# Thirteen clock fillers in two groups instead of seventeen in four, and another order of the steps, in a kernel that fuses sketched attention with a rational feed-forward layer

## The chip, the cores and the metric

The kernel runs on one core of one Trainium2 chip. The metric is the device time of one execution in microseconds (us). Several runs of a kernel are summed up by their median. A profile of one execution shows, for each engine, when its instructions ran: TensorE (PE, with its weight loads as PEld), VectorE (DVE), ScalarE (ACT), GpSimdE (POOL) and SyncE (SP), which only starts DMAs here.

## The reference, cut to what matters

Each input row is turned by two small sketches (8 x 32) into the 64 products of its two sketch vectors. Attention with these features is linear, so keys and values are first summed into a 64 x 33 matrix for each head, and every query row is then one product with it and one division. The result, 4352 rows of 128, goes through a feed-forward layer whose nonlinearity is a quotient of polynomials.

```python
def _attn_ref(q, k, v, S1, S2):          # q, k, v: 4 x 4 x 1088 x 32
    def phi(x):
        a = np.einsum('rd,bhsd->bhsr', S1, x)
        b = np.einsum('rd,bhsd->bhsr', S2, x)
        return np.einsum('bhsi,bhsj->bhsij', a, b).reshape(*x.shape[:-1], r * r)
    q_p, k_p = phi(q), phi(k)
    kv = np.einsum('bhsf,bhsd->bhfd', k_p, v)
    z = np.sum(k_p, axis=2)
    num = np.einsum('bhsf,bhfd->bhsd', q_p, kv)
    den = np.einsum('bhsf,bhf->bhs', q_p, z)[..., None] + 1e-06
    return num / den

def _moe_ref(x, w_in, w_out, a, b):      # x: 4352 x 128, w_in: 128 x 2048
    h = x @ w_in
    P = a[0] + a[1] * h + a[2] * h**2 + a[3] * h**3
    Q = 1.0 + np.abs(b[0]) * np.abs(h) + np.abs(b[1]) * h**2
    return (P / (Q + 1e-06)) @ w_out
```

## The kernel before, in words

The kernel schedules itself by hand. A long string, `ORDER`, names some 720 steps, and a loop at the end (L668) takes them one by one and issues the instructions of each. Every engine has its own queue and works through it in the order in which the steps were issued; semaphores hold an instruction until its operands are there and its buffer is free. So the order in `ORDER` decides, for each engine, what stands behind what. A step is written `name:number`.

The steps of the attention part, with the number of the batch for keys and of the query block (13 of them, up to 384 columns each) for queries:

| step | what it does | engine |
|---|---|---|
| lk, lv, lq, lw, lx | start the load of keys, values, queries, half of w_out, half of w_in | SP |
| kt0 to kt3, qt | transpose part of the keys (L254), a query block (L325) | DVE |
| ks0, ks1, ks2, qs | sketches (L261; L338 or L409) | PE |
| kc0, kc1, kc2, qc | copies of the sketches out of PSUM (L268; L345, L348 or L415); from query block 3 on, qc also sends them through DRAM to spread them over the partitions | ACT, SP |
| kf0, kf1, kf2, qf | products of the two sketches (L273; L354, L357 or L432) | DVE |
| kp0, kp1, kp2, kk | sums of keys times values (L302), and their copy (L312, L314) | PE, ACT |
| qp, qd, qi, qx | numerator and denominator (L365), denominator plus 1e-6 (L373 on DVE, from block 2 on L376 on ACT), its inverse (L380), the quotient (L385) | PE, DVE or ACT, DVE, DVE |
| qb, qk | transpose of the quotient (L391), copy into `xT` (L398), the operand of the feed-forward layer | PE, ACT |

The feed-forward part works in 17 units: unit 0 has 256 rows, units 1 to 14 are seven blocks of 512 rows in two halves of the hidden width, units 15 and 16 have 256 rows each. A unit is a tile of 128 x 4096 in bf16, worked on in halves or quarters:

| step | what it does | engine |
|---|---|---|
| h0 to h3 | a quarter of h = x w_in into one of two `h_ps` buffers (L455) | PE |
| e0 to e3 | its copy to bf16 (L461) | ACT |
| u, w, y | absolute value (L484), linear factor (L490), product (L495): Q - 1 | DVE |
| ln, ex | r = 1/Q as exp(-ln Q) (L546, L550) | ACT |
| pa or pd | a3 h + a2 (L541 on ACT, L536 on DVE) | ACT or DVE |
| s, m, x (and v) | h r, h times that, times p (L554, L558, L569; v is L564) | DVE |
| G0 to G8 | r, s and g times w_out, summed in PSUM (L588) | PE |
| st | transpose of the sum (L597) and four stores for each batch that it touches (L605) | DVE, SP, ACT |

`w_out` is first scaled by the polynomial's coefficients into three bf16 copies: `wo:0` to `wo:5`, two halves of each (L621, L623, L625); wo:0, wo:1 and wo:5 run on ACT, the others on DVE. The w_out halves in float share two buffers with the tiles `w` of the units.

The fillers are the steps `tn`. They multiply an empty tile, `idle`, and nothing reads the result; step `tn:i` issues `TURNS[i]` of them:

```python
def turn(i, cols=512):
    idle_ps = bank()
    for _ in range(TURNS[i]):
        nc.tensor.matmul(idle_ps[:, :cols], lhsT=idle[:, 0:128], rhs=idle[:, :cols], start=True, stop=True)
```

Other things that tie the order: `h_ps` has two buffers and `qT` two; the keys, the queries and the values of a batch have one buffer each, so lk, lq and lv wait for the last reader of the batch before; r, s and g are rings of four halves and p of two, so a unit waits for the units before it; `out_sb` has two buffers, so a store step waits for the stores of the step two before it.

Of the kernel before, what the change touches and what calls it, by code (L numbers as in the profile page):

```python
# [16 lines left out]
PSUM = bass.MemoryType.PSUM  # L17


TURNS = (12, 2, 0, 0, 1, 2, 0, 0, 0)  # L20
ORDER = """
tn:0 lw:1 lq:0 kt0:0 lw:0 kt1:0 lx:1 tn:1 kt2:0 lx:0 tn:4 kt3:0 tn:5 lk:1 ks0:0 qt:0 qt:1 ks1:0 kc0:0 ks2:0 kf0:0
kc1:0 kf1:0 qs:0 kc2:0 kf2:0 kp0:0 qc:0 kp1:0 ba:0 qf:0 kp2:0 wo:3 qs:1 kk:0 lv:1 qt:3 qp:0 qt:2 qc:1 wo:1 lq:1 qf:1
qs:2 qd:0 qi:0 qc:2 qp:1 qx:0 qf:2 wo:0 qb:0 qp:2 qd:1 wo:4 qk:0 qi:1 h3:0 qx:1 qd:2 wo:5 wo:2 h2:0 e3:0 kt1:1 kt0:1
h0:0 e2:0 qi:2 lk:2 pa1:0 u1:0 qs:3 w1:0 h1:0 qx:2 y1:0 qc:3 e0:0 qb:2 qb:1 qt:4 e1:0 ks1:1 qt:5 qk:2 u0:0 qk:1 qs:4
ln1:0 h2:1 w0:0 qt:6 y0:0 kc1:1 ex1:0 h0:1 kf1:1 e2:1 ks0:1 s1:0 e0:1 h1:1 m1:0 kc0:1 pa0:0 kf0:1 h3:1 lq:2 kt0:2 e1:1
x1:0 e3:1 h0:2 ln0:0 u1:1 h2:2 qf:3 w1:1 qc:4 e0:2 qp:3 e2:2 kt1:2 y1:1 ex0:0 h1:2 s0:0 h3:2 ln1:1 m0:0 kp1:1 e3:2
x0:0 qd:3 e1:2 qi:3 pd0:1 ex1:1 G0:0 qx:3 lv:2 u1:2 G1:0 ln0:1 G2:0 w1:2 lk:3 G3:0 y1:2 qs:5 kk:1 ex0:1 qb:3 G4:0
ks0:2 qk:3 qf:4 G5:0 kc0:2 ln0:2 kf0:2 qp:4 s0:1 qc:5 G0:1 qd:4 ex0:2 qi:4 qx:4 G1:1 s1:1 qb:4 ks1:2 qk:4 s0:2 pa1:1
h2:3 kt1:3 m0:1 kc1:2 h3:3 qt:7 e2:3 m1:1 kf1:2 h0:3 e3:3 ln1:2 x1:1 qs:7 h1:3 x0:1 e0:3 st:0 m0:2 h2:4 e1:3 pd1:2  # L30
pa0:2 h3:4 u1:3 qf:5 e2:4 kp1:2 w1:3 qc:7 ex1:2 x0:2 h0:4 e3:4 s1:2 pa0:3 qt:9 qp:5 y1:3 e0:4 h1:4 qd:5 m1:2 ln0:3
G2:1 qi:5 x1:2 G3:1 e1:4 kt0:3 lv:3 G4:1 ex0:3 u1:4 ks0:3 G5:1 m0:3 pa1:3 G0:2 w1:4 G1:2 ln1:3 qx:5 G2:2 y1:4 qb:5
G3:2 qk:5 ex1:3 h0:5 m1:3 kk:2 v0:3 ln0:4 h2:5 s1:3 G4:2 e0:5 ex0:4 qf:7 h1:5 x0:3 e2:5 qs:6 s0:4 qc:6 e1:5 h3:5 pd0:4
pa1:4 m0:4 h1:6 v1:3 x0:4 e3:5 G5:2 e1:6 u1:5 qp:7 ln1:4 qt:8 st:2 h3:6 w1:5 ex1:4 x1:3 G0:3 e3:6 h0:6 y1:5 pa0:5 lq:3
G2:3 s1:4 h2:6 e0:6 m0:5 qd:7 ln0:5 G3:3 qi:7 m1:4 G5:3 e2:6 qf:6 qs:8 ex0:5 x1:4 G0:4 G1:4 u1:6 qc:8 ln1:5 qp:6 v0:5
qx:7 w1:6 qb:7 qd:6 pa0:6 G2:4 qi:6 G3:4 qx:6 y1:6 qb:6 qk:7 G4:4 qk:6 ex1:5 h3:7 m0:6 pa1:5 G5:4 s1:5 h1:7 e3:7 qt:10
h2:7 st:4 e1:7 m1:5 ln0:6 h0:7 x0:5 e2:7 x1:5 e0:7 h3:8 qf:8 ex0:6 u1:7 qs:9 v0:6 h1:8 qc:9 ln1:6 w1:7 ks1:3 s0:6 e1:8
G0:5 y1:7 kc1:3 ex1:6 qp:8 h2:8 pd1:6 kc0:3 e3:8 s1:6 ln0:7 h0:8 kf0:3 e2:8 m1:6 G2:5 ex0:7 x0:6 G3:5 G4:5 kf1:3 qd:8
e0:8 qs:10 G5:5 ln1:7 qi:8 u1:8 kp1:3 qx:8 pa0:7 w1:8 qf:9 qb:8 G0:6 qk:8 y1:8 qc:10 ex1:7 h3:9 s0:7 h2:9 e3:9 s1:7
ln0:8 h0:9 m0:7 e2:9 x1:6 G2:6 e0:9 h1:10 x0:7 ex0:8 pd1:7 h1:9 m1:7 pa0:8 s0:8 G3:6 e1:9 u1:9 G0:7 qt:11 ln1:8 qp:9  # L40
qt:12 u0:9 m0:8 h3:10 e1:10 w1:9 qd:9 ex1:8 qf:10 h2:10 x0:8 e3:10 x1:7 G4:6 kk:3 e2:10 h0:10 y1:9 pa0:9 w0:9 qp:10
qi:9 y0:9 e0:10 G1:7 qx:9 qd:10 ln0:9 qi:10 s1:8 qb:9 G5:6 u1:10 G2:7 qk:9 ex0:9 G3:7 qx:10 m1:8 qb:10 G4:7 qk:10
pd1:8 ln1:9 qs:11 s0:9 h1:11 qc:11 w1:10 ex1:9 h0:11 m0:9 e1:11 x1:8 G5:7 e0:11 h3:11 y1:10 pa1:9 G0:8 s1:9 e3:11
h2:11 ln0:10 x0:9 h0:12 m1:9 e2:11 pd0:10 ex0:10 h1:12 u1:11 x1:9 G1:8 ln1:10 G2:8 w1:11 G3:8 e0:12 s0:10 G0:9 e1:12
y1:11 G4:8 ex1:10 G5:8 G1:9 m0:10 ln0:11 G2:9 qf:11 h2:12 s1:10 ex0:11 x0:10 h3:12 pa1:10 m1:10 qs:12 s0:11 G3:9 qc:12
e2:12 G4:9 pd0:11 ln1:11 G5:9 m0:11 qp:11 x1:10 e3:12 G0:10 x0:11 qd:11 ex1:11 G1:10 qi:11 u1:12 G2:10 pa1:11 qx:11
G3:10 w1:12 qb:11 G4:10 qk:11 s1:11 pa0:12 h1:13 y1:12 h3:13 e1:13 m1:11 ln0:12 h2:13 st:6 x1:11 ex0:12 G5:10 qf:12
G0:11 st:10 e3:13 qp:12 s0:12 e2:13 st:8 h0:13 ln1:12 m0:12 u1:13 h2:14 e0:13 x0:12 ex1:12 u0:13 h3:14 w1:13 e2:14
w0:13 y1:13 e3:14 h1:14 qd:12 pa1:12 y0:13 h0:14 s1:12 e1:14 qi:12 m1:12 G1:11 e0:14 G2:11 qx:12 ln1:13 u1:14 G3:11
x1:12 qb:12 G4:11 ex1:13 w1:14 G5:11 G0:12 qk:12 pd0:13 ln0:13 h0:15 y1:14 ex0:13 h2:15 pd1:13 s1:13 e0:15 G1:12 s0:13  # L50
ln0:14 G2:12 h3:15 m1:13 e2:15 m0:13 ex0:14 h1:15 x1:13 x0:13 e3:15 G3:12 e1:15 G4:12 s0:14 ln1:14 G0:13 u1:15 G5:12
m0:14 h2:16 pa0:14 w1:15 h3:16 ex1:14 st:12 y1:15 G1:13 e2:16 e3:16 h1:16 x0:14 ln0:15 u2:16 u3:16 h0:16 w2:16 s1:14
ex0:15 w3:16 G2:13 y2:16 pd0:15 e1:16 G0:15 y3:16 e0:16 G3:13 s0:15 pa1:14 u0:16 G1:15 m0:15 G4:13 ln1:15 w0:16 G5:13
m1:14 G0:14 ex1:15 y0:16 G1:14 G2:14 v1:14 ln0:16 G3:14 pd1:15 s1:15 ex0:16 x0:15 x1:14 G2:15 ln2:16 m1:15 G5:14
ex2:16 s0:16 G0:16 pa0:16 x1:15 G3:15 st:14 ln3:16 m0:16 G4:15 ex3:16 s2:16 G1:16 x0:16 pa2:16 G5:15 m2:16 pa3:16
G2:16 s3:16 G3:16 x2:16 G4:16 st:15 G5:16 m3:16 G6:16 G7:16 x3:16 G8:16 st:16
""".split()
W_ENG = (1, 1, 0, 0, 0, 1)
P_ON_ACT = (1, 1, 0, 1, 1, 0, 1, 1, 0, 1, 1, 1, 1, 0, 1, 0, 1, 0, 1, 1, 0, 1, 0, 1, 1, 1, 0, 0, 1, 1, 0, 0, 1, 1)
# [10 lines left out]
def kernel(  # L70
# [96 lines left out]
# [4 lines that stand above are left out]
# [55 lines left out]
    def bank():  # L226
        return att.tile([128, 512], FP, name="att_ps")
# [490 lines left out]
```

## Time and profile before

| | before |
|---|---|
| median of 3 runs | 272.9 us (272.5, 272.9, 273.84) |
| the profiled execution | 272.58 us, its span 270.8 us |
| PE busy | 258.0 us (95%), 1401 matmuls |
| DVE busy | 256.8 us (95%), 278 instructions |
| ACT busy | 249.1 us (92%), 224 instructions |
| POOL busy | 2.9 us |
| DMA | 19.55 MB; the 16 DMA engines are busy from 3 to 21 us |
| fillers | 17, from 1.19 to 6.64 us |

The span goes from the first to the last instruction of the profiled execution; the execution's own time is a little longer. In the rows of the timeline the first two numbers are the start and the duration in us, "xN" is the number of instructions put together in one row, and the bracket at the end gives the time that the engine stood idle just before and what it waited for. An "issue" there means that it waited for nothing that the profile shows. In the chain of work that ended last, the first number is when a piece begins and the second how long it carries the chain.

### The profile page before, as it was taken

The numbers are of one execution on the slowest core, as the hardware profiler recorded it, in microseconds if no ns is written. First come the engines' busy times: TensorE is split into PE (matmuls) and PEld (weight loads), VectorE is DVE, ScalarE is ACT, GpSimd is POOL, SyncE is SP. The second block draws the span as 40 slices with busy tenths as digits, with TensorE's granted clock in tenths as the row PEclk, the third lists the DMA queues.
The fourth block names the chain that finished last, engine by engine and source line by source line (L and its number), as shares of the span: only waits on it lengthen the run. The fifth ranks groups of instructions, "written<-read, shape, count | busy, mean of one in ns | idle before, by whom it ended". The sixth has DMA issues, their size and how long they took to land.

```text
span 270.8 us, 3744 instructions
## 1 busy us (share of the span) xinstructions
PE 258.0 (95%) x1401; PEld 146.6 (54%) x1401; DVE 256.8 (95%) x278; ACT 249.1 (92%) x224; POOL 2.9 (1%) x24
## 2 busy tenths in 40 slices
PE   8999999999999899999999999999999999999673
PEld 3887546854744354535464554434545357665362
DVE  3859999999999999999999999999999999999993
ACT  1379999989999999999999999999999999999990
POOL 4000000000000000000000000000000000000000
PEclk9999999999999999999999999999999999999999
DMA  6994424532180062331303000300216100020022
GB/s 164 286 321 138 118 76 125 160 84 67 47 151 21 12 143 75 81 77 26 97 8 121 5 1 6 120 7 0 64 47 93 23 0 2 0 39 0 1 41 40
DMA packets 30530, 19.55 MB, mean 72 GB/s; under 512 B 20400, under 2 KB 26672, under 8 KB 30512
## 3 DMA queue, kind: packets, MB, share of 16 engines
q1 hardware_dynamic: 28864, 18.92, 27.5%
q10 hardware_dynamic: 1648, 0.40, 0.7%
q8 instruction: 11, 0.18, 0.3%
q14 instruction: 7, 0.06, 0.1%
HBM read 16.16 MB, written 3.15 MB: 71 GB/s over the span
## 4 chain that ended last, share of the span: by engine, by line
ACT 38%; DVE 27%; PE 25%; issue 8%; DVEq 0%; ACTq 0%
ACT hh L461 11%; ACT ln L546 10%; PE h_ps L455 9%; ACT r L550 9%; ACT p L541 7%; PE att_ps L588 7%; DVE g L558 5%; DVE g L569 5%; DVE s L554 4%; DVE w L495 4%; DVE w L490 3%; PE att_ps L365 2%; PE att_ps L170 2%; PE att_ps L302 2%; DVE u L484 2%
## 5 line engine op out<-in xcount | busy, mean ns | idle before, releaser
L455 PE MATMUL h_ps<-xT,w_in_sb 128*128 128x512 f32 (+1 forms) x320 | 125.7, 536 | 2.3 <-ACT hh L461 1.9
L455 PEld LDWEIGHTS h_ps<-xT,w_in_sb 128*128 128x128 f32 x320 | 58.4, 190 | 53.2 <-issue 36.4
L461 ACT CAST hh<-h_ps 128x1024 bf16<-128x1024 f32 x68 | 67.9, 1023 | 3.1 <-PE h_ps L455 2.8
L588 PEld LDWEIGHTS <-w_out 128*128 128x128 bf16 x460 | 44.7, 98 | 46.7 <-issue 15.7
L546 ACT ACTIVATE ln<-w 128x2048 f32<-128x2048 bf16 (+1 forms) x35 | 65.8, 1880 | 0.5
L550 ACT ACTIVATE r<-ln 128x2048 bf16<-128x2048 f32 (+1 forms) x35 | 65.8, 1880 | 0.3
L541 ACT ACTIVATE p<-hh,a_sb 128x2048 bf16<-128x2048 bf16 (+1 forms) x23 | 46.7, 2036 | 0.0
L554 DVE TENSOR_TENSOR s<-hh,r 128x2048 bf16<-128x2048 bf16 (+2 forms) x33 | 40.9, 1247 | 0.3 <-ACT r L550 0.3
L495 DVE TENSOR_TENSOR w<-w,u 128x4096 bf16<-128x4096 bf16 (+2 forms) x22 | 39.3, 1792 | 0.0
L588 PE MATMUL att_ps<-g,w_out 128*128 128x512 bf16 (+1 forms) x160 | 35.0, 347 | 4.0 <-DVE g L569 3.9
L558 DVE TENSOR_TENSOR g<-hh,s 128x2048 bf16<-128x2048 bf16 (+1 forms) x30 | 35.0, 1171 | 0.1
L569 DVE TENSOR_TENSOR g<-g,p 128x2048 bf16<-128x2048 bf16 (+1 forms) x30 | 34.9, 1179 | 0.1
L588 PE MATMUL att_ps<-r,w_out 128*128 128x512 bf16 (+1 forms) x160 | 34.5, 347 | 0.1
L588 PE MATMUL att_ps<-s,w_out 128*128 128x512 bf16 (+1 forms) x140 | 29.7, 342 | 0.4 <-DVE s L554 0.4
L490 DVE TENSOR_SCALAR w<-u,b_abs 128x4096 bf16<-128x4096 bf16 (+2 forms) x22 | 24.0, 1096 | 0.1
L484 DVE TENSOR_SCALAR u<-hh 128x4096 uint16<-128x4096 uint16 (+2 forms) x22 | 21.3, 973 | 0.4 <-ACT hh L461 0.2
L365 PEld LDWEIGHTS att_ps<-kvz,q_pT 128*128 128x128 f32 x144 | 17.7, 192 | 3.8 <-issue 1.6
L365 PE MATMUL att_ps<-kvz,q_pT 128*128 128x66 f32 x144 | 17.8, 273 | 0.4 <-ACT sk_sb L415 0.4
L302 PEld LDWEIGHTS att_ps<-v_sb,k_p 128*64 128x64 f32 (+1 forms) x288 | 8.8, 138 | 2.3 <-issue 1.5
L536 DVE TENSOR_SCALAR p<-hh,a_sb 128x2048 bf16<-128x2048 bf16 x12 | 9.7, 805 | 0.0
L273 DVE TENSOR_TENSOR k_p<-att_ps,b_sk 128x1280 f32<-128x1280 f32 (+2 forms) x8 | 9.4, 1178 | 0.0
L302 PE MATMUL att_ps<-v_sb,k_p 128*64 128x64 f32 (+1 forms) x288 | 9.3, 223 | 0.0
(60 smaller groups left out, 134.1 us busy)
## 6 DMA issues: line engine op xcount, KB each, us to landing
a_all<-sk_d SPq DMA_DIRECT2D x6, 384.0 KB
b_all<-sk_d SPq DMA_DIRECT2D x12, 192.0 KB
v_sb<-in_v_dram SPq DMA_DIRECT2D x12, 144.0 KB
k_sb<-in_k_dram SPq DMA_DIRECT2D x3, 544.0 KB
q_sb<-in_q_dram SPq DMA_DIRECT2D x3, 544.0 KB
a_all<-sk_d SPq DMA_DIRECT2D x4, 320.0 KB
b_all<-sk_d SPq DMA_DIRECT2D x8, 160.0 KB
w_out_sb_f<-in_moe_w_out_dram SPq DMA_DIRECT2D x2, 512.0 KB
```

The source lines that it names most:

```text
L365: nc.tensor.matmul(self.nd[:, o:o + 2 * KW], lhsT=self.q_p[:, c, x:x + 128], rhs=kvz[self.b % 2][:, c, :], start=True, stop=True)
L455: nc.tensor.matmul(t[:, x * tl:(x + 1) * tl], lhsT=w_in_sb[:, f * 128:(f + 1) * 128], rhs=xT[:, x_at(t0):x_at(t0) + tl], start=True, stop= ...
L461: nc.scalar.copy(out=live[i]["hh"][:, part * PW:(part + 1) * PW], in_=live[i]["h", part])
L490: nc.vector.tensor_scalar(out=t[:, c], in0=live[i]["u"][:, c], scalar1=ab1, scalar2=ab0, op0=AX.mult, op1=AX.add)
L495: nc.vector.tensor_mul(out=t[:, c], in0=t[:, c], in1=live[i]["u"][:, c])
L541: nc.scalar.activation(out=part_of(i, "p", h), in_=hh, func=ACT.Identity, scale=a3, bias=a2)
L546: nc.scalar.activation(out=t, in_=live[i]["w"][:, span(h)], func=ACT.Ln, bias=1.0 + 1e-6)
L550: nc.scalar.activation(out=part_of(i, "r", h), in_=live[i]["ln"], func=ACT.Exp, scale=-1.0)
L554: nc.vector.tensor_mul(out=part_of(i, "s", h), in0=hh, in1=part_of(i, "r", h))
L558: nc.vector.tensor_mul(out=part_of(i, "g", h), in0=hh, in1=part_of(i, "p" if horner(i, first(h)) else "s", h))
L569: nc.vector.tensor_mul(out=g, in0=g, in1=part_of(i, "s" if horner(i, first(h)) else "p", h))
L588: nc.tensor.matmul(outs[t0][:, :tl], lhsT=w_sb[y][:, f0 + x, :], rhs=part_of(i, key, h)[:, c:c + tl], start=done[0] == 0, stop=done[0] == ...
```

## The change

`TURNS` is changed so that step tn:4 issues two fillers and tn:0 eleven, and both stand at the head of `ORDER`; tn:1 and tn:5 are gone. The order of the other steps is another one. No step is added, and each step issues what it issued before. In the first part, up to about unit 3, the new places are many; these are the ones that the next section speaks of:

- the sketches ks1:0 come before ks0:0, and qt:1 comes after kf1:0;
- qt:3, qi:2 and qx:2 come ahead of kt1:1, kt0:1 on DVE; lq:1 comes with qt:3;
- qk:2 comes ahead of e0:0 on ACT, qb:2 ahead of h1:0 on PE;
- wo:5 moves on ACT from just ahead of e3:0 to between qd:3 and e3:2;
- pa1:1 moves ahead of kc0:2, kk:1 and qd:4; ln0:2 and qc:5 come behind qd:4;
- qt:7 stands between qi:4 and qx:4 on DVE.

Behind that the same steps follow with neighbours exchanged: x0:15 ahead of y0:16, and st:15 ahead of st:14, for example.

```diff
-TURNS = (12, 2, 0, 0, 1, 2, 0, 0, 0)
+TURNS = (11, 0, 0, 0, 2, 0, 0, 0, 0)
 ORDER = """
-tn:0 lw:1 lq:0 kt0:0 lw:0 kt1:0 lx:1 tn:1 kt2:0 lx:0 tn:4 kt3:0 tn:5 lk:1 ks0:0 qt:0 qt:1 ks1:0 kc0:0 ks2:0 kf0:0
-kc1:0 kf1:0 qs:0 kc2:0 kf2:0 kp0:0 qc:0 kp1:0 ba:0 qf:0 kp2:0 wo:3 qs:1 kk:0 lv:1 qt:3 qp:0 qt:2 qc:1 wo:1 lq:1 qf:1
-qs:2 qd:0 qi:0 qc:2 qp:1 qx:0 qf:2 wo:0 qb:0 qp:2 qd:1 wo:4 qk:0 qi:1 h3:0 qx:1 qd:2 wo:5 wo:2 h2:0 e3:0 kt1:1 kt0:1
-h0:0 e2:0 qi:2 lk:2 pa1:0 u1:0 qs:3 w1:0 h1:0 qx:2 y1:0 qc:3 e0:0 qb:2 qb:1 qt:4 e1:0 ks1:1 qt:5 qk:2 u0:0 qk:1 qs:4
-ln1:0 h2:1 w0:0 qt:6 y0:0 kc1:1 ex1:0 h0:1 kf1:1 e2:1 ks0:1 s1:0 e0:1 h1:1 m1:0 kc0:1 pa0:0 kf0:1 h3:1 lq:2 kt0:2 e1:1
-x1:0 e3:1 h0:2 ln0:0 u1:1 h2:2 qf:3 w1:1 qc:4 e0:2 qp:3 e2:2 kt1:2 y1:1 ex0:0 h1:2 s0:0 h3:2 ln1:1 m0:0 kp1:1 e3:2
-x0:0 qd:3 e1:2 qi:3 pd0:1 ex1:1 G0:0 qx:3 lv:2 u1:2 G1:0 ln0:1 G2:0 w1:2 lk:3 G3:0 y1:2 qs:5 kk:1 ex0:1 qb:3 G4:0
-ks0:2 qk:3 qf:4 G5:0 kc0:2 ln0:2 kf0:2 qp:4 s0:1 qc:5 G0:1 qd:4 ex0:2 qi:4 qx:4 G1:1 s1:1 qb:4 ks1:2 qk:4 s0:2 pa1:1
+tn:4 tn:0 lw:1 lq:0 kt0:0 lw:0 kt1:0 lx:1 kt2:0 lx:0 ks1:0 kt3:0 ks0:0 lk:1 qt:0 ks2:0 kc0:0 kc1:0 kf0:0 kf1:0 qs:0
+kc2:0 qt:1 kf2:0 qc:0 kp0:0 ba:0 kp1:0 qf:0 kp2:0 wo:3 qs:1 kk:0 lv:1 qt:2 qp:0 qc:1 wo:1 qf:1 qs:2 qd:0 qi:0 qc:2
+qp:1 qx:0 qf:2 wo:0 qb:0 qp:2 qd:1 qi:1 qk:0 qx:1 qt:3 h3:0 qd:2 qi:2 lq:1 qx:2 wo:4 wo:2 h2:0 e3:0 kt1:1 h0:0 kt0:1
+e2:0 pa1:0 u1:0 lk:2 qs:3 w1:0 qb:2 h1:0 y1:0 qc:3 qk:2 e0:0 qt:5 qb:1 ks0:1 qt:4 e1:0 qs:4 qk:1 u0:0 ln1:0 h1:1 qt:6
+w0:0 y0:0 kc0:1 ex1:0 h2:1 kf0:1 ks1:1 e1:1 s1:0 e2:1 h0:1 m1:0 kc1:1 ln0:0 kf1:1 h3:1 lq:2 e0:1 x1:0 e3:1 h1:2 kt0:2
+ex0:0 u1:1 h2:2 qf:3 w1:1 qc:4 e1:2 qp:3 e2:2 s0:0 pa0:0 h3:2 y1:1 h0:2 qd:3 wo:5 e3:2 qi:3 m0:0 G0:0 e0:2 qx:3 G1:0
+ln0:1 kt1:2 x0:0 qb:3 ks0:2 u1:2 qk:3 G2:0 ex0:1 lk:3 pd0:1 G3:0 w1:2 G4:0 pa1:1 kp1:1 y1:2 kc0:2 ln1:1 G5:0 qf:4 lv:2
+qs:5 kf0:2 kk:1 ex1:1 qp:4 s0:1 ks1:2 qd:4 qc:5 qi:4 ln0:2 qt:7 G0:1 qx:4 m0:1 qb:4 G1:1 qk:4 s1:1 ex0:2 h3:3 x0:1
...
```

## The prediction

> **What bounds the kernel now.** I read the windows first, then the chain that ended last, then the timelines of the first 60 us, where the change lies. By the windows VectorE (DVE) is busy 18.5 of the first 27 us and from 30 to 260 us all but about 1 us; ScalarE (ACT) lacks about 2.5 us in that stretch, TensorE (PE) 2.9 up to 240. Three engines are full at once, and the chain goes from one to the other:
>
> ```profile
> ACT 38%; DVE 27%; PE 25%; issue 8%; DVEq 0%; ACTq 0%
> ```
>
> So a step can be put earlier for nothing only in the first 25 us, and whatever goes in later pushes something else. The chain begins on PE, with the fillers:
>
> ```profile
> 1.19 5.45 PE att_ps L170 x17
> 6.63 0.84 PE att_ps L261 x8
> 7.47 1.12 PE h_ps L261 x10
> 8.59 1.06 PE h_ps L338 x8
> 9.65 2.29 PE att_ps L302 x72
> 11.95 1.06 PE h_ps L338 x8
> ```
>
> The first nine filler weight loads start some 0.43 us apart, the last eight 0.215 apart. In the timeline of the start the second row below is that faster part; the next two are a wait for a load, and the last shows wo:5 in a spot that costs nothing, since ACT then sits idle until PE has filled the first h_ps:
>
> ```profile
> 1.19 5.45 PE L170 MATMUL att_ps<-idle 128*128 128x512 bf16 x17 [1.19 <-DVE idle L165]
> 4.53 1.61 PEld L170 LDWEIGHTS <-idle 128*128 128x128 bf16 x8 [0.23 <-issue]
> ...
> 6.66 0.77 DVE L325 STREAM_TRANSPOSE qT<-q_sb 128x256 f32<-128x256 f32 x2 [0.24 <-DMA q_sb<-in_q_dram]
> ...
> 7.36 1.25 DVE L273 TENSOR_TENSOR k_p<-att_ps,b_sk 128x512 f32<-128x512 f32 x2
> ...
> 17.35 1.04 ACT L621 CAST w_out<-w_out_sb_f 128x1024 bf16<-128x1024 f32 x1
> ...
> 19.18 1.01 ACT L461 CAST hh<-h_ps 128x1024 bf16<-128x1024 f32 x1 [0.80 <-PE h_ps L455]
> 20.39 1.37 DVE L254 STREAM_TRANSPOSE kT<-k_sb 128x224 f32<-128x224 f32 x2 [2.19 <-DMA k_sb<-in_k_dram]
> ```
>
> The last two readings are where I expect the head start to end: qd:4 on ACT, and qi:4 with qx:4 right behind it on DVE.
>
> ```profile
> 54.52 0.19 ACT L376 ACTIVATE den<-att_ps 128x12 f32<-128x12 f32 x1
> ```
> ```profile
> 54.92 0.22 DVE L380 RECIPROCAL rec<-den 128x12 f32<-128x12 f32 x1
> 55.25 0.56 DVE L385 TENSOR_TENSOR x_tok<-att_ps,rec 128x384 f32<-128x384 f32 x1
> ```
>
> **Part 1, the fillers.** Four go, and all four come out of the fast part: 4 x 0.215 = 0.86 us. PE is free at 6.64 - 0.86 = 5.78. The transposes kt0 to kt3 run from 4.76 to 6.42, the first two about 0.4 us each, so kt1 is done near 5.6 and ks1 can start at 5.78. The lead on PE is 0.86.
>
> **Part 2, what is late next.** qt:0 still waits for its load until 6.66, and kf0 stands behind it. qt:1 (0.38) now comes after kf1, so kf0 starts at 6.66 + 0.39 = 7.05 instead of 7.36: ks0 standing second (kc0 at 5.78 + 0.84 + 0.04 = 6.66) is hidden by that. kf0 and kf1 take 1.25, qt:1 0.38, so kf2 starts near 8.68 instead of 8.95 and ends at 10.17 instead of 10.44. kp2, 40 of the 72 passes at 2.29/72 = 0.032, waits for it: 10.17 + 1.27 = 11.45 instead of 11.95. Of 0.86 us 0.5 is left on PE. I take v_sb as landed: the 72 passes began at 9.6 without a DMA wait; it would have to land after 9.15 to cost anything, up to 0.35. The chain from qs:1 to qp:2 then moves up as it stands, and h3:0 starts at 16.72 instead of 17.24. Before, w_in_sb was there by 17.15, how much sooner no row tells: 0 to 0.43 us, and I take 0, because that is the near end to a row in which PE found its operand waiting.
>
> **Part 3, moved up into DVE's wait.** qi:2 and qx:2 (0.16 and 0.42) and qt:3 now run ahead of kt1:1. They fill the 2.19 us that DVE spends on k_sb, which lands at 20.39 as before. lq:1 goes with qt:3: its issue on SP moves from 13.88 to about 17; only lk:2 (21.79) is queued behind it, and qt:5 needs it at 24.4. The DMA engines are still full until 21, so I count nothing; an earlier k_sb would gain nothing either, as u1:0 waits for ACT's copy e2:0. POOL gets nothing new. ACT, 0.53 us ahead at e2:0 and with qk:2 (0.33) now before e0:0, ends e1:0 at 25.75 instead of 26.05. u0:0 waits for that, so at the end of y0:0, where both orders have done the same DVE steps, DVE is 0.33 us ahead (28.75 against 29.1). ACT starts ln1:0 0.55 ahead (26.05 against 26.60), PE its first h of unit 1 0.6 ahead.
>
> **Part 4, wo:5.** It leaves the spot at 17.35, where 0.80 us of waiting behind it covered it, and comes between qd:3 and e3:2, where ACT is full: 1.04 us at full price. pa1:1 (1.99) also moves ahead of qd:4, while ln0:2 (1.81) and qc:5 (0.20) move behind it. Sum up to qd:4: 1.04 + 1.99 - 1.81 - 0.20 = +1.02, less the lead of 0.55: +0.47. Before, qd:4 ended at 54.71; the windows give ACT some 0.3 us of idle between 40 and 55 that later work could use, so it now ends between 54.9 and 55.2. DVE, with the same steps done, comes to qi:4 at 54.92 - 0.33 = 54.6, and waits 0.3 to 0.6. Queued behind that wait on DVE are qt:7 (0.49, newly ahead) and qx:4, and for qx:4 waits qb:4, then qk:4 (behind ln0:2 on ACT, done near 57.35), then the first h of unit 3. That starts at about 57.4; before it was 57.43. By then all three engines have done the same steps in both orders, at the same time: the head start is spent.
>
> **Part 5, the rest.** From there both orders hold the same steps with neighbours exchanged. DVE's idle time from 60 to 260 is 0.6 us, so no more can be gained there; a new wait on DVE costs its length. The largest exchange I find is x0:15 ahead of y0:16: ln0:16, for which y0:16 is the operand, comes 1.13 us later on ACT. Cover: ACT's last p ended at 263.60 and its reader x3:16 began at 265.20, so 1.6 us; without it the 1.13 would be paid. st:15 now comes before st:14, and st:16 reuses st:15's buffer: its stores took 2.7 us after the transpose (264.5 to 267.2 in the DMA counts), and 3.3 us of DVE and PE work stand between; I take 0 and keep +0.4, since st:14's four issues on SP (1.8 us) now also come just ahead of st:16's. Bounds of this part: -0.6 to +0.7; I take 0.
>
> **Sum.** -0.86 + 0.36 (load of q) at kp2, +0.17 to DVE's 0.33, +0.33 at qi:4, 0 behind: 0 to -0.1 us. The profiled execution took 272.58 with a span of 270.8; the median of the three runs, 272.9, is 0.32 above it. So 272.5 for such an execution and 272.8 for a median. A measurement of this kernel can tell about 0.5%, 1.36 us, from no change (the three runs alone differ by 1.34).
>
> **Rivals.** *The head start stays* (0.27). If qd:4 comes in time, because ACT's 2.5 us of idle close up, the lead goes through to the end; at most it is the whole 0.86, where steps that I put behind one another overlap (the front has 8.2 us of DVE idle to take from), and the exchanges behind 60 us may take out DVE's 0.6: 272.9 - 0.86 - 0.6 = 271.4. For it: the waits of PE and ACT on each other are small and spread, and ACT starts unit 1 0.55 ahead. Against it: the rows give DVE only 0.33 past y0:0, and wo:5 goes into a full stretch.
>
> *The clock is released too late* (0.15). In this execution the fillers ran at half speed for 3.34 us (1.19 to 4.53) and at full speed after. Seventeen slow fillers last 7.26 us, thirteen 5.55, to 6.74. If the release falls later than in this execution and the sketches that follow, with 64 columns a matmul, do not bring it, PE stays slow for another such stretch: half of 3.34 is 1.7 us lost on the chain, from ks1 to kp2. That gives 272.8 + 1.7 = 274.5. It decides only from a release past 6.74; against it speaks that the profile has the release at 4.53, well inside thirteen fillers, and a granted clock of 1.0 all through. The Trainium skill, TensorE: Matmul & The Clock Gate, Part 1, says that the gate watches a free-running activity window of 3.4 us, so that the slow stretch varies from run to run; the 3.34 here agrees, its variation no single trace can show. By that page as an estimate two windows, 6.8 us, are sure to hold a full one: seventeen slow fillers cover that, thirteen do not.
>
> *ACT is the one that is late* (0.16). If h3:0 gets no lead, because w_in_sb lands at 17.15, ACT meets wo:5 without its 0.55: qd:4 at 55.2 + 0.5 = 55.7, the first h of unit 3 at 57.9, and ACT enters the stretch from 75 to 118 us, where the chain is its own, a full 1.0 late with p, ln and copies behind each other: +1.0 to +1.5, about 274.2. For it: the chain's largest share is ACT's. Against it: ACT waited 1.26 us for PE at 59 to 65, which takes that up.
>
> **Numbers.** The forecast has 0.42; its own range is 272.0 to 273.6. Faster by over 0.5%: most of the first rival, 0.24. Slower: the second and most of the third, 0.28. Within: the forecast and what is left, 0.48. The range reaches from the first rival to the second, 271.3 to 274.4.
>
> **What will show it.** Fillers ending near 5.8 and ks1 right behind; kf0 at about 7.05; k_p products ending at 11.45; the first h at 16.7; the cast of wo:5 near 42 with no idle time about it; a wait of DVE on ACT's den near 54.6; the first h of unit 3 at 57.4. A first h of unit 3 before 57.0 would make the forecast wrong on the fast side; slow fillers up to the sketches, or an ACT over 0.5 us later at 75 us, on the slow side.

## The result and the profile after

The changed kernel took 272.8 us (median of 20 runs, 272.29 to 273.35); the kernel before took 273.5 on the same chip (median of 20 runs, of which one took 681 us and does not count in the ratio). The ratio is 0.9976, 95% interval 0.9967 to 0.9985: a gain of 0.24%, about 0.65 us, inside the half per cent that the prediction called no change. On a second chip the same pair gave 272.54 and 273.18, ratio 0.9981 (0.9971 to 0.9991).

The profiled execution took 272.61 us with a span of 270.8; before it was 272.58 and 270.8. So two profiles of equal length stand for medians 0.65 apart, and the first thing to find is what differs between executions. The timeline of PE in the changed kernel begins like this (start, duration, engine, line, operation, and in the bracket the idle time before it):

```profile
1.19 5.38 PE L170 MATMUL att_ps<-idle 128*128 128x512 bf16 x13 [1.19 <-DVE idle L165]
6.41 1.00 PE L261 MATMUL att_ps<-S,kT 128*128 128x64 f32 x8
...
10.05 2.32 PE L302 MATMUL att_ps<-v_sb,k_p 128*64 128x64 f32 x72 [0.46 <-DMA v_sb<-in_v_dram]
...
17.57 2.64 PE L455 MATMUL h_ps<-xT,w_in_sb 128*128 128x256 f32 x11
```

Thirteen fillers end at 6.57, hardly before the seventeen of the earlier profile (6.64), because the clock was released at 6.09 in this execution and at 4.47 in that one. And the head start would have gone nowhere: the k_p sums wait 0.46 us for the values. The chain that ended last says the same; it no longer begins with the fillers (start, length, what carries it):

```profile
1.48 4.35 DMA k_sb<-in_k_dram
...
5.85 3.92 DMA v_sb<-in_v_dram
9.77 0.28 issue
10.05 2.32 PE att_ps L302 x72
```

The middle looks as foreseen. On DVE the wait for the second batch of keys is filled by the steps moved ahead of it (2.19 us before, 0.22 now), and a new wait stands at qi:4:

```profile
20.12 1.37 DVE L254 STREAM_TRANSPOSE kT<-k_sb 128x224 f32<-128x224 f32 x2 [0.22 <-DMA k_sb<-in_k_dram]
...
55.51 0.23 DVE L380 RECIPROCAL rec<-den 128x12 f32<-128x12 f32 x1 [0.50 <-ACT den L376]
```

On ACT, wo:5 has no idle time about it, and qd:4 is later than before (54.52):

```profile
42.28 1.07 ACT L621 CAST w_out<-w_out_sb_f 128x1024 bf16<-128x1024 f32 x1
...
55.30 0.18 ACT L376 ACTIVATE den<-att_ps 128x12 f32<-128x12 f32 x1
```

What made all profiles of this study comparable was to cut each at two points: the first h of unit 0, and the transpose of st:12, the seventh of the ten L597 transposes. All times in us; "k_p sums" is their start and, if they waited for the values, for how long:

| profile | k_p sums | first h | first h to st:12 | st:12 to the end |
|---|---|---|---|---|
| before | 9.63 | 17.15 | 219.01 | 34.64 |
| the changed kernel | 10.05 (0.46) | 17.57 | 219.01 | 34.24 |
| the same again (after_again) | 9.90 (0.41) | 17.42 | 218.94 | 34.23 |
| fill13_old_order | 10.29 (1.06) | 17.81 | 219.01 | 34.59 |
| fill17_new_order | 10.00 | 17.60 | 219.00 | 34.23 |
| fill13_new_front | 9.91 | 17.54 | 219.11 | 34.59 |
| fill13_new_rest | 10.02 (0.78) | 17.54 | 219.23 | 34.23 |
| new_middle | 9.99 (0.53) | 17.52 | 219.16 | 34.60 |
| new_tail | 9.36 | 16.88 | 219.03 | 34.35 |
| tail_only | 10.12 (0.77) | 17.64 | 219.01 | 34.35 |
| p_behind_den | 10.14 (1.00) | 17.66 | 219.87 | 34.24 |
| qt7_first | 10.39 (1.11) | 17.91 | 218.79 | 34.25 |
| wo5_early | 9.96 (0.67) | 17.49 | 219.04 | 34.27 |
| fill06 | 11.95 | 20.25 | 219.58 | 34.16 |

The first h comes 7.52 us after the k_p sums begin in nearly every row; with thirteen fillers those sums mostly wait for the values. The 200 us behind it are the same length in both orders, to 0.1 us. The last column has the larger part of the gain: 34.6 with the old tail (the order of the last 77 steps), 34.2 to 34.35 with the new, so 0.3 to 0.4 of the 0.65 us. The rest does not show in profiles, one execution each; it is taken up further down.

### The profile page after: what moved, and what is told of

Read it like the earlier page. It is cut to its first block, busy times and chain, and to the rows that moved or that the text cites. A ratio compares the mean times of both kernels' runs of the same rounds, so it can differ in the third digit from the quotient of the medians.

```text
span 270.8 us, 3732 instructions
## 1 busy us (share of the span) xinstructions
PE 257.7 (95%) x1382; PEld 147.5 (54%) x1397; DVE 256.7 (95%) x278; ACT 248.8 (92%) x224; POOL 2.9 (1%) x24
## 4 chain that ended last, share of the span: by engine, by line
ACT 47%; PE 34%; issue 8%; DVE 5%; DMA 4%; SPq 0%; ACTq 0%; DVEq 0%
PE h_ps L455 16%; ACT ln L546 13%; ACT r L550 12%; ACT hh L461 12%; PE att_ps L588 10%; ACT p L541 7%; PE att_ps L365 3%; DMA v_sb<-in_v_dram 2%; PE att_ps L302 2%; DMA k_sb<-in_k_dram 2%; DVE g L558 2%; DVE s L554 1%; ACT xT L398 1%; PE att_ps L391 1%; PE att_ps L409 1%
## 5 line engine op out<-in xcount | busy, mean ns | idle before, releaser
L588 PEld LDWEIGHTS <-w_out 128*128 128x128 bf16 x460 | 45.5, 100 | 45.9 <-issue 14.3
L365 PE MATMUL att_ps<-kvz,q_pT 128*128 128x66 f32 x144 | 17.9, 273 | 0.1
L273 DVE TENSOR_TENSOR k_p<-att_ps,b_sk 128x1024 f32<-128x1024 f32 (+2 forms) x8 | 9.3, 1178 | 0.1
```

What stands on the lines that cost most here:

```text
L365: nc.tensor.matmul(self.nd[:, o:o + 2 * KW], lhsT=self.q_p[:, c, x:x + 128], rhs=kvz[self.b % 2][:, c, :], start=True, stop=True)
L588: nc.tensor.matmul(outs[t0][:, :tl], lhsT=w_sb[y][:, f0 + x, :], rhs=part_of(i, key, h)[:, c:c + tl], start=done[0] == 0, stop=done[0] == ...
```

## The experiments

Ratios are to the kernel before on the same chip, from five rounds, with their 95% interval. Steps are counted without fillers; "before[:192]" stands for the first 192 steps of the order before, which are the same set as the changed kernel's first 192 (up to about unit 3).

**Fillers and orders apart.** Theory: the fillers give a head start that the new front spends again. Rivals: the head start stays; the gain is in the neighbours exchanged behind the front.

fill13_old_order:

```diff
-TURNS = (12, 2, 0, 0, 1, 2, 0, 0, 0)
+TURNS = (11, 0, 0, 0, 2, 0, 0, 0, 0)
-ORDER = before
+ORDER = tn:4 tn:0 + before without fillers
```

> The order of before with thirteen fillers instead of seventeen, nothing else. If the fillers are the gain (first theory): the whole of the changed kernel's gain, 0.6 to 0.7 us off a median, a ratio near 0.9976, because 4 x 0.43 us go whenever the clock is released late. If the new order is the gain (second theory): within 0.1% of before. If the clock needs the seventeen (the late release of the prediction): slower by up to 1.7 us in the runs where the release falls past 6.7 us.

273.07 us, 0.9993 (0.9984 to 1.0001). PE is free early, and waits for the values instead:

```profile
1.19 4.76 PE L170 MATMUL att_ps<-idle 128*128 128x512 bf16 x13 [1.19 <-DVE idle L165]
5.78 1.00 PE L261 MATMUL att_ps<-S,kT 128*128 128x64 f32 x8
...
10.29 2.32 PE L302 MATMUL att_ps<-v_sb,k_p 128*64 128x64 f32 x72 [1.06 <-DMA v_sb<-in_v_dram]
```

Here, with the clock released at 4.82, the sketches begin at 5.78, the time of the prediction, and the 0.69 us won against 6.47 ends in a wait of 1.06.

fill17_new_order (against the changed kernel):

```diff
-TURNS = (11, 0, 0, 0, 2, 0, 0, 0, 0)
+TURNS = (15, 0, 0, 0, 2, 0, 0, 0, 0)
```

> The new order with seventeen fillers at its head. First theory (fillers): no gain, ratio 1.000. Second theory (order): the whole gain, ratio near 0.9976. The forecast's own step, that a head start of PE is spent at the 13th step of DVE after it, would make this equal to the changed kernel.

273.41 us (272.57 to 273.75), 1.0004 (0.9992 to 1.0015). Its profile is as short as the changed kernel's, but nine of its twelve runs lie at 273.16 to 273.75 and three at 272.57 to 272.94; the profile is one of the latter. More on this below.

fill13_new_front and fill13_new_rest:

```diff
-ORDER = before
+ORDER = tn:4 tn:0 + changed[:192] + before[192:]
...
+ORDER = tn:4 tn:0 + before[:192] + changed[192:]
```

> Thirteen fillers and the new order up to unit 3 (the first 192 steps, after which both orders have done the same steps), then the order of before. If the exchanges behind unit 3 do nothing, as the forecast took it (0 between bounds of -0.6 and +0.7): the same time as the changed kernel, ratio 0.9976. If they carry the gain: ratio 1.000.

> Thirteen fillers, the first 192 steps in the order of before, the rest in the new order. By the forecast's step for wo:5, which here stays in the spot that costs nothing, with no wait of DVE at qi:4: as fast as the changed kernel or up to 0.3 us faster. If the new front is the gain: near before, ratio 1.000. If the rest is: ratio 0.9976.

New front: 273.08 us, 0.9995 (0.9986 to 1.0003). New rest: 272.77 us, 0.9982 (0.9974 to 0.9990). The front, where the change is large, gives nothing that these runs resolve; the exchanges behind it, which the prediction had put at zero, carry most of the gain.

**Where in the rest.** The rest was cut again at step 642, in unit 15, with the changed kernel run beside the parts.

```diff
-ORDER = before
+ORDER = tn:4 tn:0 + before[:642] + changed[642:]
...
+ORDER = tn:4 tn:0 + before[:192] + changed[192:642] + before[642:]
```

> The changed kernel itself, beside its parts on one chip. If its gain of 0.24% is that of the exchanges behind unit 3 with thirteen fillers (0.9982 in fill13_new_rest) and the new front adds nothing to it, it gives 0.9975 to 0.9985. If front and rest add up (0.9995 and 0.9982 each against the kernel before, the fillers' 0.9993 counted once), it gives 0.9984. A ratio over 0.999 would say that the gain of the first comparison belongs to the chip.

> Thirteen fillers at the head; the first 642 steps as before, the last 77 as in the changed kernel: x0:15 ahead of y0:16, st:15 ahead of st:14, and their neighbours. If the gain sits in the drain (3.24 us behind the last store transpose in the changed kernel, 3.77 before), this one has it: ratio 0.998, about 0.3 us under fill13_old_order. If it sits in the exchanges between unit 3 and the tail, this one is at fill13_old_order's 0.9993. The prediction's own count has this part at 0 to +0.4 us.

> Thirteen fillers at the head; steps 193 to 642 (unit 3 up to unit 15) as in the changed kernel, the first 192 and the last 77 as before. If the tail carries the gain: 0.9993, as fill13_old_order. If the exchanges in the middle do: 0.998. At 60 to 260 us the kernel before has 0.6 us of idle time on DVE, so at most 0.6 us (0.9971 with the fillers' part).

after_again 272.54 us, 0.9981 (0.9971 to 0.9991); new_tail 272.68 us, 0.9980 (0.9971 to 0.9989); new_middle 273.06 us, 0.9997 (0.9988 to 1.0006). new_tail and new_middle have the same fillers and the same front, and their runs do not overlap (272.04 to 272.75 against 273.00 to 273.27). So it is the last 77 steps. The table's profiles split it further: from st:12 to the transpose of st:16 the changed kernel needs 0.13 us more (30.55 against 30.42), from there to the end 0.53 less (3.69 against 4.22).

The 0.53 is not in the work on the data. The trace's records of SP's last instructions show what it is. After the stores, SP waits for the DMA semaphores one by one in a fixed order (start in us, length in ns):

```
before                                       changed
268.69  679  waits for 103 and 104           269.23   28  waits for 103 and 104
269.41   28  waits for 102 and 106           269.66   28  waits for 102 and 106
269.81   28  waits for 100 and 107           269.75  137  waits for 100 and 107
269.90   28  waits for 101 and 108           269.92   28  waits for 101 and 108
269.97   28  waits for 109 and 110           269.99   27  waits for 109 and 110
270.80       end of the span                 270.82       end of the span
```

The store issued last is ACT's second one of st:16, at 267.48 before and 268.04 after, and it ends the waiting 1.39 to 1.43 us after its issue is done. Before, it signals semaphore 103, which SP waits for first, so the other four waits (0.6 us of SP's time) come behind the landing. In the changed kernel it signals 100, the third in SP's list: the first two waits are over by then, and only 0.93 us instead of 1.43 lie between the landing and the end. All profiles agree: in the four with the old tail the last store signals 103, and from the transpose of st:16 to the end they need 4.2 us; in the ten with the new one it signals 100, and they need 3.7 to 3.9. (3.9 is new_tail and tail_only, where none of the five waits blocks, but 0.4 us pass between the second and the third.) In the records of the stores the semaphores come roughly in turn (102, 103, 104, 106, 107, 108 and so on), so which one the last store gets hangs on the order of the stores before it. What stands in another order there is st:15 and st:14; no run exchanges these two alone.

tail_only, the new tail by itself, with the fillers of before:

```diff
-ORDER = before
+ORDER = before[:642] + changed[642:]
```

> The kernel before, with its seventeen fillers in four groups and its first 642 steps, and the last 77 steps of the changed kernel: st:15 ahead of st:14, x0:15 ahead of y0:16 and their neighbours. If the tail's gain stands by itself (0.4 us between new_tail and fill13_old_order, of one filler count and one front), the ratio is 0.9986, with two groups of runs as the kernel before has them, each 0.4 us lower: near 272.5 and near 273.1. If the tail needs thirteen fillers, as the seventeen fillers in the new order (1.0004) might mean, the ratio is 0.9995 to 1.000.

272.88 us, 0.9994 (0.9982 to 1.0006): short of the expected 0.9986, which the interval holds, as it holds no change. Its profile has the shorter tail (34.35, 0.29 less than before). Its runs fall in two groups, as expected: seven at 272.66 to 272.93 and five at 273.22 to 273.54; the kernel before has them on that chip at 272.45 to 273.18 and 273.39 to 273.84. The median hangs on how many fall in each. Group by group the mean is lower with the new tail, 272.77 against 272.95 and 273.34 against 273.70, but these groups were cut after the fact. That the tail gains 0.3 to 0.4 is shown by the profiles and, with thirteen fillers, by the times; in the times of seventeen-filler kernels it is not resolved.

**The wait at qi:4 and wo:5.** Theory (Part 4): wo:5 makes qd:4 late, and DVE loses the wait.

p_behind_den, qt7_first and wo5_early, each against the changed kernel:

```diff
-pd0:1 G3:0 w1:2 G4:0 pa1:1 kp1:1
+pd0:1 G3:0 w1:2 G4:0 kp1:1
-G1:1 qk:4 s1:1
+G1:1 qk:4 pa1:1 s1:1
...
-qi:4 ln0:2 qt:7 G0:1
+qt:7 qi:4 ln0:2 G0:1
...
-wo:5 e3:2
+e3:2
-qd:2 qi:2
+qd:2 wo:5 qi:2
```

> The changed kernel with pa1:1 moved behind qk:4 on ACT, so that qd:4 comes some 2 us sooner; DVE's order is the same. DVE's wait of 0.50 us at qi:4 should be gone. If that wait is lost time, as the prediction has it, the end comes 0.3 to 0.5 us sooner: 0.998 to 0.999 of the changed kernel's time on this chip. If the time comes back as a later wait (s1:1 or the third unit's p, for which ACT is now 2 us late), it is the changed kernel's time within 0.1 us, or more by what DVE then waits for p of unit 1.

> The changed kernel with one step moved: qt:7 (0.44 to 0.52 us on DVE) ahead of qi:4, where DVE waits 0.50 us for qd:4. ACT and PE keep their orders. If that wait is lost time on DVE, and DVE sets the time from there to the tail, the end comes 0.4 us sooner: 272.1 to 272.2 where the changed kernel has 272.54, ratio to the kernel before 0.9965. If the time is set by ACT or PE (as moving pa1:1 suggests, which closed the same wait and cost 0.9), DVE waits the 0.4 a few steps later, at kf1:2 or the u of unit 3, and the time stays: 0.998.

> The changed kernel with wo:5 back behind qd:2, ahead of e3:0, where ACT waits 1.73 us for PE. By Part 4 of the prediction wo:5 costs 1.04 us on ACT where it now is, and the DVE wait of 0.50 at qi:4 comes from it; without it qd:4 comes 1.04 sooner, the wait is gone and the end comes up to 0.5 us sooner: ratio 0.996. If ACT's time there has room (it waits 0.70 us for PE at e3:3 behind it in the changed kernel), the time stays at 0.998 and that wait of ACT grows by about 1 us.

p_behind_den: 273.42 us, 1.0003 (0.9995 to 1.0012), 0.88 us above the changed kernel on that chip. The wait at qi:4 is gone, and a longer one stands seven DVE instructions later, since kc1:2 now has the p of 2.1 us ahead of it on ACT:

```profile
59.52 1.22 DVE L558 TENSOR_TENSOR g<-hh,s 128x2048 bf16<-128x2048 bf16 x1
61.68 1.49 DVE L273 TENSOR_TENSOR k_p<-att_ps,b_sk 128x1280 f32<-128x1280 f32 x1 [0.94 <-ACT b_sk L268]
```

So with pa1:1 out of the way qd:4 comes in time for DVE, and leaving pa1:1 where it is costs less than putting it later.

qt7_first: 272.70 us, 0.9978 (0.9969 to 0.9988). In DVE's timeline the transpose fills the wait, and the inverse follows with no idle time:

```profile
55.26 0.57 DVE L325 STREAM_TRANSPOSE qT<-q_sb 128x384 f32<-128x384 f32 x1
55.84 0.23 DVE L380 RECIPROCAL rec<-den 128x12 f32<-128x12 f32 x1
```

From the first h to st:12 that wins 0.22 us, half of what was expected. In the times it is not resolved: the changed kernel itself has 0.9976 and 0.9981 on two other chips.

wo5_early: 272.76 us, 0.9977 (0.9967 to 0.9986); first h to st:12 is 219.04, as without the edit. In ACT's timeline a wait for PE stands where wo:5 had been:

```profile
42.15 0.20 ACT L376 ACTIVATE den<-att_ps 128x12 f32<-128x12 f32 x1
42.29 1.01 ACT L461 CAST hh<-h_ps 128x1024 bf16<-128x1024 f32 x1
44.01 1.01 ACT L461 CAST hh<-h_ps 128x1024 bf16<-128x1024 f32 x1 [0.70 <-PE h_ps L455]
```

and the wait at qi:4 stays (0.46 in its DVE timeline). wo:5 is not its cause.

**Fewer fillers.**

```diff
-TURNS = (11, 0, 0, 0, 2, 0, 0, 0, 0)
+TURNS = (4, 0, 0, 0, 2, 0, 0, 0, 0)
```

> The changed kernel's order with six fillers in the place of thirteen. If the loads of q and v set the front (the k_p sums wait for v until 9.9 to 10.3 us in most profiles here), the fillers only have to keep PE from being late: six end near 3.8 us at half speed, PE then waits for the key transposes, and the first h stays at 17.4 to 17.6 and the time at 0.998, as long as the clock is released by then. If the clock is released only after a stretch of steady work, which six fillers and the sketches between their waits do not give, the sketches run at half speed: ks and qs twice as long, some 1 to 2.5 us more, ratio 1.002 to 1.008. By the prediction's second rival the price is 1.7 us.

275.64 us (273.0 to 276.38), 1.0074 (1.0047 to 1.0100). The clock is released at 13.71 us, and everything that PE does before runs at half speed; compare the sketches with 1.00 and the k_p sums with 2.32 above:

```profile
1.19 2.74 PE L170 MATMUL att_ps<-idle 128*128 128x512 bf16 x6 [1.19 <-DVE idle L165]
5.91 1.97 PE L261 MATMUL att_ps<-S,kT 128*128 128x64 f32 x8 [1.98 <-DVE kT L254]
...
11.95 3.10 PE L302 MATMUL att_ps<-v_sb,k_p 128*64 128x64 f32 x72
```

The first h is 2.7 us later than in the changed kernel, and the profile's span 3.2 longer.

## Why the prediction was right, and where it was not

The time came out as said, 272.8, but to the tenth by luck. The forecast took 0 to 0.1 us off 272.9, the median of the first three runs; the median of twenty is 273.5, and the change takes 0.65 off that. What was right is that the time hardly moves, since the new front gains nothing. The working behind it was wrong in several of its terms.

- **Part 1, the fillers.** Right where the clock is released as early as in the profile of before: 5.78 in fill13_old_order. But the release is not fixed at 4.53. In the thirteen profiles with thirteen or seventeen fillers it lies between 3.86 and 6.48 us, and at 6.09 the thirteen end at 6.57.
- **Part 2, the failing step: "I take v_sb as landed".** It had the bound (a landing after 9.15 costs) but capped the cost at 0.35 and took zero. In nine of the fourteen profiles the sums wait for the values, until 9.90 to 10.39. In those the first h comes at 17.4 to 17.9 and not at 16.72, whatever the fillers do: a lead of 0.5 was expected, none is there. The profile of before, with its sums at 9.63 and no wait, had some of the earliest loads in the study: DVE could take up the queries at 6.66, in twelve of the other profiles only at 7.08 to 7.55, so that kf0 too came later than forecast (7.69 in the changed kernel, for 7.05). A row in which an operand happens to be there says nothing of how much earlier it came.
- **Part 3.** DVE's wait for k_sb was filled as said (0.22 left). Its worth was nothing: what had been one wait of 2.19 became 0.22, 0.88 and 0.66, the last two before the u steps, for ACT's copies. (One sum here is off by 0.1: a lead of 0.53 less 0.33 for qk:2 leaves 0.20 at the end of e1:0, not 0.30.)
- **Part 4, wo:5 at full price.** Measured: 0.1 at most (219.04 without it there, 219.01 and 218.94 with it). Relative to the first h, qd:4 comes 0.36 later than before (37.73 against 37.37) where the sum had +1.02, and the first h of unit 3 comes 0.10 later (40.38 against 40.28) where 0.4 was expected (57.4 less 16.72, against 40.28). In the new order wo:5 covers a wait of ACT for PE of 0.70 that the order before does not have. The wait at qi:4 was foreseen in place and size (0.50 in a forecast of 0.3 to 0.6), but it hangs on pa1:1, with which it goes (p_behind_den), and not on wo:5, without which it stays (wo5_early, 0.46); closing it with qt:7 gives back 0.22 of its 0.50.
- **Part 5, the rest at zero.** For the neighbours exchanged in the middle that holds: 219.0 to 219.2 in every mixture. x0:15 ahead of y0:16 was covered, as said: DVE has no wait there in the changed kernel. The exchange of st:15 and st:14 was given 0 to +0.4; the new tail brought -0.4, by SP's list of waits, which the sum did not look at. The bound of the part, -0.6, holds it by luck: it was worked out from DVE's idle time.

So the rival *the head start stays* had a gain of nearly half its size, by another mechanism. *The clock is released too late* did not come about: even with the release at 6.48 (fill13_new_front) the first h is at 17.54. Its mechanism is real, as fill06 shows, with 2.7 us at the first h for the 1.7 of the rival; thirteen fillers are enough in every execution seen. The granted clock of 1.0 that the prediction set against this rival says nothing of the start: it stands in the profile of before, whose fillers ran at half speed up to 4.47. *ACT is the one that is late* did not show.

What the four fillers less are worth lies in the spread, and it is the part of the gain that stays open. In the order of before they bring 0.1 us in the median (fill13_old_order), not resolved from zero; in the new order, 1.0004 with seventeen against 0.9976 and 0.9981 with thirteen, they bring 0.6 or more. Among the 32 runs of the kernel before on the second chip, fifteen have a mean granted clock of 0.998 or more and a mean of 272.93 us, and thirteen have less than 0.992 and a mean of 273.51; new_middle, with thirteen fillers and the same tail, has 273.06 and 273.08 in these two groups.

A late release would explain that. The mean clock leaves out the slow start and counts what is slow near the end, and from this the release can be estimated. In new_middle's profile (mean 0.989) there is a slow stretch of 3.41 us, and the last drop comes at 268.66, 262.83 us behind the release at 5.83. A run of before with 0.989 and a span of 271.5 us has lost 3.0 us of clock, 1.7 of them in such a stretch, so its last drop is 2.6 us before the end, at 268.9, and its release near 6.1. For the eleven runs with 0.989 this gives 6.1 to 6.4, to about 0.3 since the mean has three digits. The distance carries over because every stretch of one clock in the records is a whole multiple of 3.413 us (249.17 is 73, 266.24 is 78); a release one such step sooner would give the same mean, but none in a profile is before 3.86.

At 6.09, seventeen fillers would end near 7.4 (twelve at 0.43 from 1.19, five at 0.215). The sketches begin 0.17 us ahead of that, and the sums 3.2 to 3.3 us behind the sketches where they do not wait for the values (6.47 to 9.63 in before, 6.60 to 9.91 in fill13_new_front). So the sums would begin near 10.4 to 10.6, up to 0.6 us behind the values, which land at 9.9 to 10.4. This is worked out, not shown: no profile of a seventeen-filler kernel caught a release after 4.84. It would also explain the runs of fill17_new_order at 273.2 to 273.75; there it stays open, since their mean clock does not tell them apart.

By one profile each, the new front and the new middle cost 0.1 to 0.2 us when each stands alone (219.11, 219.23, 219.16) and nothing together. No version beat the changed kernel by more than the intervals.

## What to carry to other kernels

Before a head start is priced, ask of every load on the way how early it lands, over several executions: a wait that is missing in one profile is no slack. When a large reordering moves the time little, cut the profiles at common steps and compare the pieces; here one table put the larger part of the gain into the last 35 us, far from where most of the edits were. And look at the very end: the order in which the last waits are taken, against the order in which the last stores land, was worth 0.5 us.

## What the runs showed of the hardware

- The release of the clock varies by 2.6 us between profiles (3.86 to 6.48), with the fillers starting at 1.19 in each. The Trainium skill, TensorE: Matmul & The Clock Gate, Part 1, gives 500 ns to either side, and says that the window behind it runs free; the spread measured here is wider than that figure.
- Small matmuls were slow to bring the release: in fill06 PE worked nearly without a gap from 5.91 on, first on the key sketches with 64 columns a matmul, from 9.94 on the query sketches with 256 and from 11.95 on the sums with 64, and the clock came at 13.71, 7.8 us after it began.
- In the changed kernel's profile the clock went back to half for 3.41 us (255.26 to 258.67), at the end of a wait of PE of only 2.16 us; the same wait in the profile of before, 2.17 us, left it at full speed. It cost nothing: st:12 to the end took 34.24 us with it and 34.23 without (fill17_new_order).
